# A planned three-engine kernel: the first layer's low product moves from GpSimd to VectorE, with two buffers for low parts, one-bank sums and a new order

## The chip, the cores and the metric

The kernel runs on one core of one Trainium2 chip. The metric is the device time of one execution in microseconds (us), and the time before is the median of three runs. One more execution was recorded by the hardware profiler; its trace is what is read here. The engines are called PE (TensorE, the matrix engine; PEld is its weight load), DVE (VectorE), ACT (ScalarE), POOL (GpSimd) and SP (SyncE, which here issues every DMA).

## What is computed

A causal weighted average over 7 positions (softmax of `weight` for each of 8 heads), then two feed-forward layers of width 2048 over 8192 tokens of 192 values. The first has a rational activation, the second a squared ReLU.

```python
x = attn(x, weight)                       # 7-tap causal average, 2 x 4096 tokens, 192 wide
h = x @ moe_w_in                          # 8192 x 192 @ 192 x 2048
P = a[0] + a[1]*h + a[2]*h*h + a[3]*h*h*h
Q = 1.0 + abs(b[0])*abs(h) + abs(b[1])*h*h
x = (P / (Q + 1e-6)) @ moe_w_out          # 8192 x 2048 @ 2048 x 192
h = x @ moe2_w_in
g = s * relu(h)**2 + b
out = g @ moe2_w_out
```

## The kernel before

**Tiling.** Tokens go in 16 blocks of 512 (`NB`); the 2048 hidden columns go in 8 chunks of 256 (`NPAIR`), so each layer has 16 x 8 = 128 chunks, numbered i (first layer) and j (second). A hidden chunk is a tile of 128 partitions x 2 x 512.

**High and low parts.** Matmuls run in the format fp32r. To keep more digits, each operand is split into a high part (rounded to fp32r) and a low part (what the rounding left). Each chunk of either layer has 10 matmuls into the hidden tile (`mm_in`, L482 to L494) and 10 out of it (`mm_out`, L496 to L503): 6 with the high part of the hidden value and 4 with its low part. Each has 512 columns.

**The first layer's chunk** (`first`, L506 to L607), by engine. PE: `in1`. ACT: `V` (L516), `B` (L530), `S` (L522), `Ln` (L549), `Exp` (L552), which give the numerator's square, the denominator Q and its reciprocal R. DVE: `v` (L540, the numerator; it is the last reader of the hidden PSUM tile and frees it), `hi` (L557, the high part), `m` (L563) and `rest` (L569), which give what the high part missed, multiplied by Q. POOL: `lo` (L575), that remainder times R, which is the low part. PE: `oh` and `ol` (L499) add the high and the low products to the block's sums. The tile `lo` has one buffer, so the `lo` of chunk i waits for the `ol` of chunk i - 1; Q, R and V have three buffers each, and `lo` is the last reader of Q and R.

**The second layer's chunk** (`second`, L671 to L711): `in2` on PE; `relu` (L680), `hi2` (L684) and `Sq` (L687) on ACT; `lo2` (L691, a subtraction) on DVE, into one buffer; `oh2` and `ol2` on PE.

**Between them.** The sums of a block are a PSUM tile of two banks, `acc1` for the first layer and `acc2` for the second, one of each. `middle` (L609 to L668) reads `acc1` and makes the operands of the second layer: `half` (L617) and `middle high` (L626) on ACT, `add` (L632) and `middle low` (L642) on DVE, `mid high` (L650) on ACT, `mid low` (L658) on DVE, one copy by DMA. `finish` (L713 to L747) reads `acc2`: `f1` (L720) and `f0` (L727) on ACT, `other` (L736) on DVE, two stores. The other two hidden tiles `h0` and `h1` take the remaining four of the eight PSUM banks; either layer's `in` takes the one that is free.

**Ahead of it.** For each block the 7 taps (L370, L372) and the split of x (L379, L380, L392, L393) run on DVE and ACT. At the start the 16 weight chunks are loaded as 64-bit floats, read as integer words, and converted to high and low parts (`convert`, L274 to L344) on ACT and DVE. `choose` (L749 to L763) is 14 very short DVE instructions that set a flag: whether the fast form used here holds for the given coefficients. The flag is read at the very end (L931), and a second, general program follows only if it does not hold. While PE has nothing to do at the start it runs 18 + 240 fill matmuls on zeros (L822).

**What sets the order.** Each engine runs its instructions in the order of the program. That order comes from a planner (`Plan.order`, L117 to L166): every step has an engine, a cost and predecessors, and the planner takes, engine by engine, among the steps that can start within `window` of the earliest, the one with the smallest key: chunk number x `PERIOD` plus a constant for its kind (`KEY`). Steps marked `two`, and all POOL steps, also exclude each other in its clock (`port`). So the keys only decide among steps that are ready at nearly the same planned moment. In between, semaphores enforce the dependences of tiles: a reader waits for the last writer of a tile, and a writer for its last readers.

Of the kernel before, what the change touches and what calls it, by code (L numbers as in the profile page):

```python
# [65 lines left out]
PERIOD = 49.3361  # L66
SAME, OTHER, WINDOW = 0.13, 0.18, 0.0346
KEY = {
    "B": -205.47, "Exp": 1361.10, "Ln": -1099.73, "S": 2329.47, "Sq": -1965.35, "V": -35.99,
    "add": 76.87, "again2": 3213.31, "bias": 250.60, "choose": 0.00, "f0": -476.58,  # L70
    "f1": -346.45, "fill": 1302.02, "finish": -1057.72, "flatten": 1033.64, "half": 533.91,
# [4 lines left out]
    "mid low": -600.72, "middle high": 1011.40, "middle low": -55.44, "oh": 399.83,  # L76
    "oh2": 956.49, "ol": 208.83, "ol2": 363.40, "raw": 217.36, "relu": -316.51,
    "rest": -215.80, "rows": 55.35, "store": -645.27, "store2": -35.28, "tap0": 706.19,
# [3 lines left out]
}  # L82
WARM, FILLS = 18, 120
MOST, WORST, SMALL, LARGE = 0.5, 16.0, 1e-6, 1e12
# [85 lines left out]
def conv_rational_relu2(  # L170
# [30 lines left out]
    def part(nm, n):  # L201
        return work.tile([P, 2, NB], F32R, tag=nm, name=nm, bufs=n)

# [292 lines left out]
    def mm_out(acc, W, x, c, terms):  # L496
        for k in range(2):
            for n, (w, m) in enumerate(terms):
                nc.tensor.matmul(  # L499
                    acc[:, m, :], lhsT=W[c][:, w + k * P:w + (k + 1) * P], rhs=x[:, k, :],  # L500
                    start=terms is HIGH and c == 0 and k == 0 and n != 1,
                    stop=terms is LOW and c == NPAIR - 1 and k == 1,
                )  # L503


    def first(i, x_done):  # L506
# [66 lines left out]
        def low(_):  # L573
            lo = a["lo"] = part("lo", 1)
            nc.gpsimd.tensor_tensor(lo, a["q"], a["r"], op=ALU.mult)  # L575

        def out_high(_):
            if c == 0:
                accs[1, blk] = psum("acc1")
# [13 lines left out]
        else:  # L593
# [10 lines left out]
        s_lo = step("lo", i, "Pool", 2.4, i, low, (s_r, ("ol", i - 1)))  # L604
        s_oh = step("oh", i, "PE", 6 * MM, i, out_high,
                    (s_h, ("lows", c), ("middle low", blk - 1) if c == 0 else None))
        return step("ol", i, "PE", 4 * MM, i, out_low, (s_lo, s_oh))  # L607

    def middle(blk, ready):  # L609
# [4 lines left out]
        def half(tag):  # L614
            a["t"] = scratch(tag)[0:D1]
            if fast:
                nc.scalar.activation(  # L617
                    a["t"], accs[1, blk][D1:P, 1, :], AF.Copy, scale=sign[D1:P]
                )
                return  # L620
            nc.scalar.copy(a["t"], accs[1, blk][D1:P, 1, :])

        def high(_):
            X2[blk] = x_tiles(2)
            if fast:
                nc.scalar.activation(X2[blk][0], accs[1, blk][:, 0, :], AF.Copy, scale=sign)  # L626
                return
            nc.scalar.copy(X2[blk][0], accs[1, blk][:, 0, :])

        def add(_):  # L630
            if fast:
                nc.vector.scalar_tensor_tensor(  # L632
                    a["t"], accs[1, blk][0:D1, 1, :], sign[0:D1], a["t"],
# [3 lines left out]
            nc.vector.tensor_add(a["t"], accs[1, blk][0:D1, 1, :], a["t"])  # L637

        def low(_):
            xh, xl, _, _ = X2[blk]  # L640
            if fast:
                nc.vector.scalar_tensor_tensor(  # L642
                    xl, accs[1, blk][:, 0, :], sign, xh.bitcast(F32),
# [3 lines left out]
            nc.vector.tensor_sub(xl, accs[1, blk][:, 0, :], xh.bitcast(F32))  # L647
# [8 lines left out]
        def low2(_):  # L656
# [333 lines left out]
```

## Time and profile before

| | us |
|---|---|
| median of 3 runs (lowest to highest) | 1298.39 (1295.28 to 1298.67) |
| the profiled execution | 1297.07 |
| its span, first to last instruction | 1295.2 |
| PE busy | 1245.9 (96%) |
| ACT busy | 1175.8 (91%) |
| DVE busy | 1087.8 (84%) |
| POOL busy | 382.8 (30%) |

The profiled execution lasts 1.87 us longer than its span and 1.32 us less than the median. Its granted TensorE clock was 0.992 of the full 2.4 GHz on average. A busy share is an average over stages that have different limits, so the stretches are read one by one in the rows below. A matmul's own duration (0.39 us) is longer than the distance at which the next one starts, since matmuls are pipelined; PE is therefore counted in starts. Likewise a DVE or ACT instruction overlaps the next one's start a little, so a group's busy sum is larger than the engine's busy time.

### The profile page before, as it was taken

Reading aid. Unit: us, or ns where it says so; the run is one execution under the profiler, and the core shown is the slowest. Engines: PE = TensorE matmul, PEld = TensorE weight load, DVE = VectorE, ACT = ScalarE, POOL = GpSimd, SP = SyncE. Lnnn points to the kernel's source line nnn. Section 1 sums busy time; section 2 is a strip of 40 time slices with the busy share of each in tenths; the row PEclk is TensorE's granted clock in tenths of the full one; section 3 lists DMA queues with packets and bytes.
Section 4 is the critical chain, followed back from the end, with each engine's and each line's share of the span. In section 5 each row is a group of like instructions: output and inputs, shape, how many; then the busy total and the mean of one; then the engine's idle time right before and its main releaser. Section 6 shows DMA issues by size and latency. Waiting matters only on the chain.

```text
span 1295.2 us, 14466 instructions
## 1 busy us (share of the span) xinstructions
PE 1245.9 (96%) x5405; PEld 985.1 (76%) x5414; DVE 1087.8 (84%) x1038; ACT 1175.8 (91%) x1241; POOL 382.8 (30%) x160
## 2 busy tenths in 40 slices
PE   7989999999999999999989999899999999999997
PEld 3555787788888888787778787787877778888885
DVE  7999998999889989998878778787878887887832
ACT  4989999999999999989979899799979999999864
POOL 1122223324232232323242332433243232323300
PEclk8999999999999999999999999999999999999999
DMA  5410010000000100000000000000000000000000
GB/s 196 183 49 5 1 29 17 13 25 13 6 25 9 29 13 13 25 13 17 9 25 5 13 17 14 21 5 13 17 13 17 1 17 5 17 1 5 13 17 15
DMA packets 12047, 30.32 MB, mean 23 GB/s; under 512 B 1792, under 2 KB 1792, under 8 KB 11968
## 3 DMA queue, kind: packets, MB, share of 16 engines
q1 hardware_dynamic: 11968, 29.32, 7.4%
q8 instruction: 44, 0.72, 0.2%
q14 instruction: 35, 0.29, 0.1%
HBM read 18.96 MB, written 6.29 MB: 19 GB/s over the span
## 4 chain that ended last, share of the span: by engine, by line
PE 60%; ACT 17%; DVE 13%; issue 5%; POOL 4%; DMA 0%; ACTq 0%; DVEq 0%; POOLq 0%
PE acc L499 30%; PE h L490 30%; POOL lo L575 4%; ACT R L549 2%; ACT Q L522 2%; ACT Q L530 2%; ACT hi L684 2%; ACT V L516 2%; DVE V L540 2%; DVE Q L563 2%; DVE hi L557 1%; DVE y L372 1%; DVE Q L569 1%; ACT R L552 1%; ACT G L687 1%
## 5 line engine op out<-in xcount | busy, mean ns | idle before, releaser
L575 POOL TENSOR_TENSOR lo<-Q,R 128x1024 fp32r<-128x1024 f32 x128 | 376.6, 2942 | 848.9 <-PE acc L499 357.2
L499 PE MATMUL acc<-hi,w 128*128 128x512 f32 x1536 | 380.7, 390 | 4.1 <-DVE hi L557 2.4
L499 PEld LDWEIGHTS acc<-hi,w 128*128 128x128 f32 x1536 | 287.4, 188 | 68.2 <-DVE hi L557 4.4
L499 PE MATMUL acc<-lo,w 128*128 128x512 f32 x1024 | 266.9, 392 | 8.0 <-POOL lo L575 6.7
L499 PEld LDWEIGHTS acc<-lo,w 128*128 128x128 f32 x1024 | 191.1, 188 | 54.7 <-POOL lo L575 12.3
L691 DVE TENSOR_TENSOR lo<-G,hi 128x1024 fp32r<-128x1024 f32 x128 | 174.9, 1366 | 54.9 <-PE acc L499 32.8
L557 DVE SCALAR_TENSOR_TENSOR hi<-V,few,R 128x1024 fp32r<-128x1024 f32 x128 | 166.4, 1300 | 49.2 <-PE acc L499 25.1
L540 DVE SCALAR_TENSOR_TENSOR V<-V,few,h 128x1024 f32<-128x1024 f32 x128 | 163.2, 1276 | 51.7 <-ACT Q L530 51.4
L563 DVE SCALAR_TENSOR_TENSOR Q<-Q,few,hi 128x1024 f32<-128x1024 f32 x128 | 190.5, 1488 | 2.5
L490 PE MATMUL h<-x1h,w 128*128 128x512 f32 x512 | 165.4, 405 | 21.0 <-DVE V L540 11.1
L569 DVE SCALAR_TENSOR_TENSOR Q<-V,few,Q 128x1024 f32<-128x1024 f32 x128 | 183.9, 1436 | 0.6
L680 ACT ACTIVATE G<-h 128x1024 f32<-128x1024 f32 x128 | 130.3, 1018 | 41.7 <-PE h L490 27.7
L530 ACT ACTIVATE Q<-h,few 128x1024 f32<-128x1024 f32 x128 | 142.3, 1112 | 28.2 <-POOL lo L575 27.6
L516 ACT ACTIVATE V<-h,few 128x1024 f32<-128x1024 f32 x128 | 153.5, 1199 | 8.3 <-PE h L490 7.7
L490 PE MATMUL h<-x2h,w 128*128 128x512 f32 x512 | 158.5, 391 | 2.6 <-DVE V L540 2.6
L549 ACT ACTIVATE R<-Q,few 128x1024 f32<-128x1024 f32 x128 | 146.9, 1148 | 1.2
L522 ACT ACTIVATE Q<-Q,few 128x1024 f32<-128x1024 f32 x128 | 147.1, 1149 | 0.9
L552 ACT ACTIVATE R<-R,few 128x1024 f32<-128x1024 f32 x128 | 146.9, 1148 | 1.0
L684 ACT ACTIVATE hi<-G 128x1024 fp32r<-128x1024 f32 x128 | 135.4, 1058 | 4.0 <-PE acc L499 3.3
L687 ACT ACTIVATE G<-G 128x1024 f32<-128x1024 f32 x128 | 135.1, 1055 | 0.7
L490 PEld LDWEIGHTS h<-x1h,w 128*128 128x128 f32 x512 | 94.3, 190 | 52.6 <-ACT G L680 11.7
L490 PEld LDWEIGHTS h<-x2h,w 128*128 128x128 f32 x512 | 94.9, 188 | 24.7 <-DVE V L540 3.5
(101 smaller groups left out, 1393.2 us busy)
## 6 DMA issues: line engine op xcount, KB each, us to landing
raw<-w SPq DMA_DIRECT2D x16, 767.8 KB, 7.0
x_in<-xt SPq DMA_DIRECT2D x24, 259.0 KB, 2.7
out<-z SPq DMA_DIRECT2D x16, 256.0 KB, 2.0
x2d<-x2d SPq DMA_DIRECT2D x16, 128.0 KB, 2.2
out<-z SPq DMA_DIRECT2D x16, 128.0 KB, 2.3
x1d<-x1d SPq DMA_DIRECT2D x15, 128.0 KB, 2.2
head<-taps SPq DMA_DIRECT2D x1, 11.0 KB, 1.8
```

The costliest lines, as they stand in the source:

```text
L490: nc.tensor.matmul(h[:, k, :], lhsT=W[c][:, w + k * P:w + (k + 1) * P], rhs=x, start=terms is wide and n == 0, stop=terms is rest and n == ...
L499: nc.tensor.matmul(acc[:, m, :], lhsT=W[c][:, w + k * P:w + (k + 1) * P], rhs=x[:, k, :], start=terms is HIGH and c == 0 and k == 0 and n ...
L516: nc.scalar.activation(a["v"], a["h"], AF.Square, bias=alpha, scale=slope)
L522: nc.scalar.activation(a["q"], a["q"], AF.Square, bias=beta)
L530: nc.scalar.activation(a["q"], a["h"], AF.Abs, scale=root)
L540: nc.vector.scalar_tensor_tensor(v, v, cadd if fast else ab[:, 1:2], a["h"], op0=ALU.add, op1=ALU.mult)
L549: nc.scalar.activation(a["r"], a["q"], AF.Ln, bias=lnb, scale=2.0 ** -QEXP)
L557: nc.vector.scalar_tensor_tensor(hi, a["v"], padd if fast else ab[:, 0:1], a["r"], op0=ALU.add, op1=ALU.mult)
L563: nc.vector.scalar_tensor_tensor(q, q, qadd if fast else qc, a["hi"].bitcast(F32), op0=ALU.add, op1=ALU.mult)
L569: nc.vector.scalar_tensor_tensor(q, a["v"], padd if fast else ab[:, 0:1], q, op0=ALU.add, op1=ALU.subtract)
L575: nc.gpsimd.tensor_tensor(lo, a["q"], a["r"], op=ALU.mult)
L691: nc.vector.tensor_sub(lo, a["g"], a["hi"].bitcast(F32))
```

## The change

- `lo` of every chunk of the first layer is issued on DVE (`nc.vector`) instead of POOL (`nc.gpsimd`), with the planner's cost 1.14 instead of 2.4. POOL then has no work after the start.
- `lo` and `lo2` get two buffers each (`LOWS = 2`), and wait for the `ol` or `ol2` two chunks back instead of one.
- `acc1` and `acc2` become two tiles of one bank each. Their readers' predecessors follow: `middle high` and `half` each wait only for the sums, `add` for `half`, `middle low` for `middle high`, and `f0` no longer waits for `f1`. The first `oh` of a block also waits for `add` of the block before.
- `choose` gets the key of chunk 128 instead of 32, waits for `finish` of block 0, and is registered behind all other steps.
- `PERIOD`, `WINDOW` and all of `KEY` are new, so the planner gives a new order on every queue.

`RELU_ON_DVE` is empty, so `relu` stays on ACT. The general program keeps one buffer and POOL; it gets the one-bank sums too.

```diff
-PERIOD = 49.3361
-SAME, OTHER, WINDOW = 0.13, 0.18, 0.0346
+PERIOD = 153.1447
+SAME, OTHER, WINDOW = 0.13, 0.18, 0.0993
 KEY = {
...
 WARM, FILLS = 18, 120
+LOWS = 2
+RELU_ON_DVE, LOW_ON_DVE = (), (0,1,2,3,4,5,6,7)
...
+    def sums(tag):
+        return [ps.tile([P, NB], F32, tag=f"{tag}{m}", name=f"{tag}{m}") for m in range(2)]
+
     def psum(tag):
         return ps.tile([P, 2, NB], F32, tag=tag, name=tag)
...
         def low(_):
-            lo = a["lo"] = part("lo", 1)
-            nc.gpsimd.tensor_tensor(lo, a["q"], a["r"], op=ALU.mult)
+            lo = a["lo"] = part("lo", LOWS if fast else 1)
+            engine = nc.vector if fast and c in LOW_ON_DVE else nc.gpsimd
+            engine.tensor_tensor(lo, a["q"], a["r"], op=ALU.mult)
 
         def out_high(_):
             if c == 0:
-                accs[1, blk] = psum("acc1")
+                accs[1, blk] = sums("acc1")
             mm_out(accs[1, blk], W1, a["hi"], c, HIGH)
...
-        s_lo = step("lo", i, "Pool", 2.4, i, low, (s_r, ("ol", i - 1)))
+        own = fast and c in LOW_ON_DVE
+        s_lo = step("lo", i, "DVE" if own else "Pool", 1.14 if own else 2.4, i, low, (s_r, ("ol", i - (LOWS if fast else 1))), two=True)
         s_oh = step("oh", i, "PE", 6 * MM, i, out_high,
-                    (s_h, ("lows", c), ("middle low", blk - 1) if c == 0 else None))
+                    (s_h, ("lows", c), *((("add", blk - 1), ("middle low", blk - 1)) if c == 0 else ())))
...
         hs = step("middle high", blk, "ACT", 0.48, when, high,
-                  [t] + [("in2", NPAIR * (blk - 1) + c) for c in range(NPAIR)])
-        ad = step("add", blk, "DVE", 0.6, when, add, (hs,))
-        ls = step("middle low", blk, "DVE", 0.6, when, low, (ad,))
-        h2 = step("mid high", blk, "ACT", 0.52, when, high2, (ad,))
+                  [ready] + [("in2", NPAIR * (blk - 1) + c) for c in range(NPAIR)])
+        ad = step("add", blk, "DVE", 0.6, when, add, (t,))
+        ls = step("middle low", blk, "DVE", 0.6, when, low, (hs,))
+        h2 = step("mid high", blk, "ACT", 0.52, when, high2, (hs, ad))
...
-        s_l = step("lo2", j, "DVE", 1.14, j, low, (s_s, ("ol2", j - 1)), two=True)
+        s_l = step("lo2", j, "DVE", 1.14, j, low, (s_s, ("ol2", j - (LOWS if fast else 1))), two=True)
...
-        f0 = step("f0", blk, "ACT", 0.66, when, most, (f1,), take="scratch")
+        f0 = step("f0", blk, "ACT", 0.66, when, most, (ready, ("bias", 0)), take="scratch")
...
-        if fast:
-            step("choose", 0, "DVE", 2.5, 4 * NPAIR, choose)
         for blk in range(NBLK):
...
+        if fast:
+            step("choose", 0, "DVE", 2.5, NPAIR * NBLK, choose, (("finish", 0),))
         for st in plan.order():
```

## Rows read from the trace of the kernel before

**Rows 1.** Windows: busy us (x instructions) of PE, PEld, DVE, ACT, POOL; clock; DMA.

```profile
22.50:50.00 27.50, 23.04 (x87) 13.56 (x88) 27.02 (x45) 24.92 (x38) 0.92 (x1) 0.84 0.47 178
50.00:100.00 50.00, 45.92 (x196) 27.17 (x198) 49.12 (x61) 45.45 (x60) 14.26 (x6) 1.00 0.24 89
100.00:190.00 90.00, 86.18 (x388) 63.54 (x391) 88.92 (x104) 87.19 (x106) 23.35 (x9) 1.00 0.05 13
300.00:500.00 200.00, 199.80 (x878) 163.77 (x877) 182.80 (x165) 195.18 (x199) 61.13 (x22) 1.00 0.06 15
500.00:1100.00 600.00, 581.75 (x2517) 471.28 (x2516) 492.44 (x441) 551.10 (x559) 196.81 (x63) 0.99 0.05 14
```

**Rows 2.** Chain of waits, PE work without idle time: start, us, what.

```profile
326.49 4.53 PE acc L499 x20
```

**Rows 3.** Line view, PE's fills: count, ns min/median/max, first and last start.

```profile
L822 PE MATMUL acc<-G x249: 379/379/650, 1.2 to 137.7; 128*128 128x512 bf16 x125
```

**Rows 4.** Timeline of DVE at the start: start us, duration us, instruction.

```profile
3.83 0.17 DVE L858 TENSOR_TENSOR head<-head,few 128x14 f32<-128x14 f32 x1
...
10.02 0.48 DVE L370 TENSOR_SCALAR y<-x_in,head 128x512 f32<-128x512 f32 x1
...
16.94 1.01 DVE L306 SCALAR_TENSOR_TENSOR z<-top,z 128x768 int16<-128x768 int16 x1
```

**Rows 5.** Tile view of x_in in the first 40 us: issue to landing.

```profile
DMA to landing us min/median/max: 2.6/2.9/3.3
```

**Rows 6.** Timeline of ACT at the start: the first weight chunk.

```profile
9.41 0.90 ACT L294 ACTIVATE z<-raw 128x768 int32<-128x768 uint32 x1
```

**Rows 7.** Timeline of DVE: a low product of the second layer and its follower.

```profile
198.59 1.22 DVE L691 TENSOR_TENSOR lo<-G,hi 128x1024 fp32r<-128x1024 f32 x1
199.73 1.28 DVE L569 SCALAR_TENSOR_TENSOR Q<-V,few,Q 128x1024 f32<-128x1024 f32 x1
```

**Rows 8.** The page's costliest groups: busy us, mean ns, idle before, its releaser.

```profile
L575 POOL TENSOR_TENSOR lo<-Q,R 128x1024 fp32r<-128x1024 f32 x128 | 376.6, 2942 | 848.9 <-PE acc L499 357.2
...
L691 DVE TENSOR_TENSOR lo<-G,hi 128x1024 fp32r<-128x1024 f32 x128 | 174.9, 1366 | 54.9 <-PE acc L499 32.8
...
L563 DVE SCALAR_TENSOR_TENSOR Q<-Q,few,hi 128x1024 f32<-128x1024 f32 x128 | 190.5, 1488 | 2.5
...
L569 DVE SCALAR_TENSOR_TENSOR Q<-V,few,Q 128x1024 f32<-128x1024 f32 x128 | 183.9, 1436 | 0.6
```

**Rows 9.** Line views of two DVE lines, columns as in group 3.

```profile
L691 DVE TENSOR_TENSOR lo<-G,hi x128: 1204/1220/3207, 142.1 to 1283.4; 128x1024 fp32r<-128x1024 f32 x128
...
L563 DVE SCALAR_TENSOR_TENSOR Q<-Q,few,hi x128: 1266/1280/3472, 45.8 to 1225.7; 128x1024 f32<-128x1024 f32 x128
```

**Rows 10.** Timeline of POOL: a product near the start.

```profile
58.42 2.39 POOL L575 TENSOR_TENSOR lo<-Q,R 128x1024 fp32r<-128x1024 f32 x1 [6.59 <-DVE Q L569]
```

**Rows 11.** Timeline of DVE: the instruction that meets it.

```profile
59.63 2.27 DVE L563 SCALAR_TENSOR_TENSOR Q<-Q,few,hi 128x1024 f32<-128x1024 f32 x1
```

**Rows 12.** Windows of two places, columns as in group 1.

```profile
640.00:680.00 40.00, 35.78 (x149) 28.41 (x148) 30.58 (x30) 33.12 (x35) 14.97 (x4) 0.96 0.10 27
948.00:988.00 40.00, 35.80 (x155) 28.50 (x154) 30.53 (x31) 33.76 (x35) 15.34 (x4) 1.00 0.07 20
```

**Rows 13.** Timeline of POOL: the product in the first of these places.

```profile
653.80 8.12 POOL L575 TENSOR_TENSOR lo<-Q,R 128x1024 fp32r<-128x1024 f32 x1 [11.81 <-ACT R L549]
```

**Rows 14.** Timeline of ACT: who waited for it, idle time in brackets.

```profile
661.95 1.12 ACT L530 ACTIVATE Q<-h,few 128x1024 f32<-128x1024 f32 x1 [4.15 <-POOL lo L575]
```

**Rows 15.** Waits: engine line waited for, us in total, times, longest.

```profile
DVE lo L691 <- PE acc L499: 32.8, 32, 4.1
...
PE h L490 <- DVE V L540: 13.7, 9, 1.9
```

**Rows 16.** Chain of waits at the end: start, us, what.

```profile
1279.54 2.56 PE acc L499 x10
```

**Rows 17.** Timeline of DVE at the end, idle time in brackets.

```profile
1287.54 0.74 DVE L736 SCALAR_TENSOR_TENSOR z<-acc,head,z 64x512 f32<-64x512 f32 x1 [2.91 <-ACT z L727]
```

More of the change, by code (lines that the diff above doesn't have):

```diff
@@ L65 @@
 }
-PERIOD = 49.3361
-SAME, OTHER, WINDOW = 0.13, 0.18, 0.0346
+PERIOD = 153.1447
+SAME, OTHER, WINDOW = 0.13, 0.18, 0.0993
 KEY = {
-    "B": -205.47, "Exp": 1361.10, "Ln": -1099.73, "S": 2329.47, "Sq": -1965.35, "V": -35.99,
-    "add": 76.87, "again2": 3213.31, "bias": 250.60, "choose": 0.00, "f0": -476.58,
-    "f1": -346.45, "fill": 1302.02, "finish": -1057.72, "flatten": 1033.64, "half": 533.91,
[4 rows of a table removed]
-    "mid low": -600.72, "middle high": 1011.40, "middle low": -55.44, "oh": 399.83,
-    "oh2": 956.49, "ol": 208.83, "ol2": 363.40, "raw": 217.36, "relu": -316.51,
-    "rest": -215.80, "rows": 55.35, "store": -645.27, "store2": -35.28, "tap0": 706.19,
[3 rows of a table removed]
+    "B": 2065.15, "Exp": 1765.52, "Ln": -517.70, "S": 110.85, "Sq": -1729.37, "V": 2437.89,
+    "add": 1443.98, "again2": 854.45, "bias": -96.78, "choose": -4317.30, "f0": 2690.75,
+    "f1": -1796.18, "fill": 770.95, "finish": -689.17, "flatten": -3154.65, "half": -320.53,
[4 rows of a table added]
+    "mid low": -246.78, "middle high": -273.37, "middle low": -636.70, "oh": 893.43,
+    "oh2": 2518.06, "ol": 368.02, "ol2": 2702.40, "raw": -276.87, "relu": -2491.34,
+    "rest": 2392.24, "rows": -3516.19, "store": 916.79, "store2": 123.89, "tap0": 1361.44,
[3 rows of a table added]
 }
 WARM, FILLS = 18, 120
+LOWS = 2
+RELU_ON_DVE, LOW_ON_DVE = (), (0,1,2,3,4,5,6,7)
 MOST, WORST, SMALL, LARGE = 0.5, 16.0, 1e-6, 1e12
@@ L617, in half @@
                 nc.scalar.activation(
-                    a["t"], accs[1, blk][D1:P, 1, :], AF.Copy, scale=sign[D1:P]
+                    a["t"], accs[1, blk][1][D1:P], AF.Copy, scale=sign[D1:P]
                 )
                 return
-            nc.scalar.copy(a["t"], accs[1, blk][D1:P, 1, :])
+            nc.scalar.copy(a["t"], accs[1, blk][1][D1:P])
         def high(_):
@@ L625, in high @@
             if fast:
-                nc.scalar.activation(X2[blk][0], accs[1, blk][:, 0, :], AF.Copy, scale=sign)
+                nc.scalar.activation(X2[blk][0], accs[1, blk][0][:], AF.Copy, scale=sign)
                 return
-            nc.scalar.copy(X2[blk][0], accs[1, blk][:, 0, :])
+            nc.scalar.copy(X2[blk][0], accs[1, blk][0][:])
         def add(_):
@@ L636, in add @@
                 return
-            nc.vector.tensor_add(a["t"], accs[1, blk][0:D1, 1, :], a["t"])
+            nc.vector.tensor_add(a["t"], accs[1, blk][1][0:D1], a["t"])
         def low(_):
@@ L646, in low @@
                 return
-            nc.vector.tensor_sub(xl, accs[1, blk][:, 0, :], xh.bitcast(F32))
+            nc.vector.tensor_sub(xl, accs[1, blk][0][:], xh.bitcast(F32))
         def high2(_):
@@ L679, in relu @@
             a["g"] = tmp("G", 2)
+            if fast and c in RELU_ON_DVE:
+                nc.vector.tensor_scalar(a["g"], a["h"], 0.0, None, op0=ALU.max)
+                return
             nc.scalar.activation(a["g"], a["h"], AF.Relu)
@@ L689, in low @@
         def low(_):
-            lo = a["lo"] = part("lo2", 1)
+            lo = a["lo"] = part("lo2", LOWS if fast else 1)
             nc.vector.tensor_sub(lo, a["g"], a["hi"].bitcast(F32))
@@ L694, in out_high @@
             if c == 0:
-                accs[2, blk] = psum("acc2")
+                accs[2, blk] = sums("acc2")
             mm_out(accs[2, blk], W2, a["hi"], c, HIGH)
@@ L702, in second @@
                  list(x_done) + [("weights", NPAIR + c)], take="slot")
-        s_r = step("relu", j, "ACT", 0.9, j, relu,
+        own = fast and c in RELU_ON_DVE
+        s_r = step("relu", j, "DVE" if own else "ACT", 1.14 if own else 0.9, j, relu,
                    (h, ("lo2", j - 2), ("fill", FILLS - 1) if j == 1 else None), free=(h,))
@@ L720, in half @@
             nc.scalar.activation(
-                a["t1"], accs[2, blk][D1:P, 1, :], AF.Identity,
+                a["t1"], accs[2, blk][1][D1:P], AF.Identity,
                 bias=bias2[D1:P, 1:2], scale=ss[D1:P],
@@ L727, in most @@
             nc.scalar.activation(
-                a["t0"], accs[2, blk][:, 0, :], AF.Identity, bias=bias2[:, 0:1], scale=ss
+                a["t0"], accs[2, blk][0][:], AF.Identity, bias=bias2[:, 0:1], scale=ss
             )
@@ L736, in other @@
             nc.vector.scalar_tensor_tensor(
-                t1, accs[2, blk][0:D1, 1, :], ss[0:D1], t1, op0=ALU.mult, op1=ALU.add
+                t1, accs[2, blk][1][0:D1], ss[0:D1], t1, op0=ALU.mult, op1=ALU.add
             )
@@ L817, in conv_rational_relu2 @@
         nc.vector.memset(idle, 0.0)
-        zero = psum("acc2")
+        zero = sums("acc2")[0]
         def fill(n):
@@ L822, in fill @@
                 nc.tensor.matmul(
-                    zero[:, 0, :], lhsT=idle[:, 0:P], rhs=idle, start=True, stop=True
+                    zero, lhsT=idle[:, 0:P], rhs=idle, start=True, stop=True
                 )
```

6 lines of the change are left out of this document (3 added, 3 removed), and 14 rows, old and new, of the table KEY.

## The prediction

> **What bounds the kernel now.** I read the windows first. From 300 to 500 us PE is busy 199.8 of 200 us [rows 1]: there it is the bound. Twenty of its matmuls take 4.53 us [rows 2], so one costs 0.2266 us, and 200 us hold 883. The 5120 matmuls of the two layers (128 chunks x 20 x 2) need 5120 x 0.2266 = 1160 us. No part of the change touches these. So the question is what lies around the 1160 us, in a span of 1295.2.
>
> Two stretches hold most of it. In the head, from 22.5 to 190 us, DVE is the fullest engine: 27.02, 49.12 and 88.92 us busy, which is 165.1 of 167.5 (98.5%) [rows 1]; PE looks busy only because 249 recorded fills run until 137.7 us [rows 3]. The head ends when DVE has converted the weights and served the first blocks. In the steady part, 500 to 1100 us, PE starts 2517 matmuls where 600 / 0.2266 = 2648 would fit: 131 missing, 29.7 us. Its idle time there is 18.3 us [rows 1]; the rest is unrecorded matmuls and a clock below full (0.99). So 18 to 30 us are to be had there.
>
> **Where the steady loss sits.** Two windows of 40 us (of three that look alike, some 154 us apart) start 149 and 155 matmuls instead of 176.5, so they lose 6.2 and 4.9 us [rows 12]; with the third (149, as the first) that is 17.3 us. In the first of them one POOL product takes 8.12 us [rows 13]. ACT waits 4.15 us for it, as the tile Q is not free until then [rows 14]. DVE then gets Q late, PE gets the hidden tile late, and the granted clock of the window is 0.96, while in its like at 948 it stays at 1.00 [rows 12]: the pause costs PE its idle time and in two of three cases some slow matmuls behind it.
>
> **POOL and DVE disturb each other.** A product on POOL runs from 58.42 to 60.81 us [rows 10]. A DVE instruction of line 563 that starts at 59.63 takes 2.27 us [rows 11] where the median is 1.28 [rows 9], and so ends 1.1 us after POOL does. The mean of line 563 is 1.488 against that median: 128 x 0.208 = 26.6 us. Line 691 loses 128 x (1.366 - 1.220) = 18.7, line 569 (same form as 563) 128 x (1.436 - 1.280) = 20.0 [rows 8, 9]. These three lines alone lose 65 us of DVE time to POOL. The 2.9 us that POOL needs per product [rows 8] against 2.39 [rows 10] show the other direction.
>
> **The change part by part.**
>
> *The product on DVE.* The nearest row is line 691: two SBUF inputs, the same shape and types. It takes 1.22 us, and the next instruction starts 1.14 us after it [rows 7]. Bounds: 1.14 and 1.28 (line 563, an instruction with one more operation); I take 1.14. DVE gains 128 x 1.14 = 146 us and loses at least the 65 above: 1088 + 146 - 65 = 1169 us at most, 92% of a span of 1270. PE stays the bound on average, but barely above DVE.
> - In the head there are 1 + 6 + 9 = 16 products [rows 1], +18.2 us on the fullest engine. Each met about one stretched instruction; at the 1.0 us of [rows 11] that returns 16. Net +2 us, bounds 0 (more returned than I count) and +18 (nothing returned).
> - In the steady part DVE has 600 - 492 = 108 us free [rows 1]; 63 products add 72. I put no cost on them; the cover is that idle time, and where it is gone each product costs 1.14 us (the slower rival).
> - The three places above disappear: -17, bounds 0 and -30. What is late next is DVE's line 540, which frees the hidden tile: PE waits for it 9 times, 13.7 us [rows 15]. Some of these waits are in the three places.
>
> *A new wait on DVE.* `lo` needs a buffer that `ol` has left. On POOL that wait (357 us [rows 8]) held up nobody; on DVE, behind it stand line 540, `hi` and the taps. Its likeness is line 691, which with one buffer waits 32.8 us for PE in 32 cases [rows 15]. With two buffers for both, the wait is for the chunk before last; I take 0, bounds -33 and +33 us of DVE idle time, which touches PE only when DVE is the fullest.
>
> *`choose` later.* After line 858 ends at 4.00 us, DVE does nothing but `choose` and its waits until the first tap at 10.02: 6.0 us [rows 4]. The first x tile is issued by 1.2 us or so and lands within 3.3 us [rows 5], so the taps could start at 4.5. The first conversion also needs ACT's line 294, which ends at 10.31 [rows 6], while DVE's join (line 306) starts at 16.94 [rows 4], six taps and more behind. So the head can start 5.5 us earlier. I take -5; bounds 0 (another load is late) and -6. Behind block 0 its 14 short instructions lie in DVE's idle time. If that is missing they cost 3 us; nobody waits for the flag before the end.
>
> *One-bank sums, two buffers at the end.* The last chunks have ten matmuls in 2.56 us instead of 2.27 [rows 2, 16], as the one buffer of `lo2` holds them: with three such chunks, -0.9. The last DVE instruction waits for line 727 [rows 17], which the split lets it pass: -0.8. Bounds 0 and -2. Inside, the split lets line 632 go before 626; it is covered by PE work.
>
> *The new order.* It moves everything on every queue, also SP's loads, copies and stores. Loads of x land in 3 us [rows 5] and a block takes 8 x 20 x 2 x 0.2266 = 72.5 us, so a transfer has room in either order. The rows of before can't show the order itself. What speaks for it: planned costs for DVE are right to a few per cent, while the planner's POOL step (2.4 us) could take 8.12 [rows 13]; without POOL the chip should follow the plan more closely. That the order loses nothing new in the head is an assumption.
>
> **The sum**, against the profiled execution: 1297.07 - 5 (choose) + 2 (head) - 17 (three places) - 1.7 (end) = 1275.4; I say 1275. The median before was 1.3 us above that execution, inside the spread of the runs.
>
> **The rivals.**
> 1. *The order gains more.* All 30 us of the steady loss go, choose gives 6, the head pays nothing, the end 1.7: 1297.1 - 37.7 = 1259. For it: 300 to 500 us already ran without loss with DVE at 91%. Against it: there DVE still had POOL to take the products, and not all of PE's waits for line 540 lie in those three places.
> 2. *The gain is given back in the head.* Only half of the stretches return, as the products fill the places where DVE sat beside POOL: +18.2 - 8 = +10; the steady part saves 4 instead of 17, since the waits for line 540 take over; 1297.1 - 5 + 10 - 4 - 1.7 = 1296. No measurable change.
> 3. *DVE becomes the bound: slower.* DVE's queue is in order. If `lo` stands ahead of line 540, the hidden tile is freed 1.14 us later and PE waits. At two chunks of eight in all blocks that is 32 x 1.14 = 36.5 against the 21.7 of the sum: 1312. It decides from 21.7 / 1.14 = 19 chunks of 128 on. For it: at 300 to 500 us DVE has 17.2 us free [rows 1] and 22 products of 1.14 are 25 us, so without returned stretches it would be over full there; line 540 is already what PE waits for most. Against it: those stretches do return, at least 22 x 65 / 128 = 11 us of them, which leaves DVE at 98% in the densest stretch and well below elsewhere. The Trainium skill (Perfetto Trace Analysis, Optimizing Scalar/DVE Operations) speaks on this side: with DVE saturated, moving some of its work to GpSimd may make sense, and this change does the reverse. The same section doubts the offload between these two because they share a read port, and the stretched row above shows that sharing.
>
> **How the numbers follow.** Forecast (1275, itself between 1264 and 1289): 0.54. Rival 1: 0.17. Rival 2: 0.12. Rival 3: 0.17. About 0.3% (4 us) is what a measurement of this kernel can tell from no change. Faster 0.71, same 0.12, slower 0.17. The range runs from 1255, a little under rival 1, to 1307, short of rival 3's centre: outside lie about half of rival 3 and little below.
>
> **What would show it.** POOL idle behind the first 10 us. Median and mean of lines 563, 569 and 691 equal. `lo` at 1.22 us on DVE. First tap at about 4.5 us, and the fills over by 132 us or so. No window of 40 us between 500 and 1100 that starts fewer than 165 matmuls. DVE busy between 1140 and 1170 us. Wrong it would be if PE's waits for line 540 grow well beyond 13.7 us, if DVE waits for PE in the new `lo` with a queue behind it, or if the head lasts longer with DVE still full.

## The result: 1254.7 us, twice the forecast gain

| | before | after |
|---|---|---|
| median, us | 1297.74 (1295.28 to 1298.67) | 1254.72 (1254.61 to 1255.00) |
| profiled execution, us / span | 1297.07 / 1295.2 | 1254.61 / 1252.7 |
| ratio, 95% interval | | 0.9672 (0.9655 to 0.9688) |
| DVE busy, us | 1087.8 | 1143.6 |
| matmul starts, 500 to 1100 us | 2517 | 2647 |

43 us were gained where 22 were forecast. The direction and the mechanism held; the size did not, and the missing half is the subject of the experiments. Line numbers are higher after the change: `lo` is L581 (575 before), `v` L545 (540), `hi` L562 (557), `m` L568 (563), `rest` L574 (569), `lo2` L701 (691).

The page after, engines first (busy us, share, instructions), then its costliest groups (busy us, mean ns | idle time before), which answer [rows 8]:

```profile
span 1252.7 us, 14124 instructions
...
PE 1231.3 (98%) x5405; PEld 986.6 (79%) x5414; DVE 1143.6 (91%) x1166; ACT 1187.6 (95%) x1241; POOL 13.5 (1%) x32
...
L701 DVE TENSOR_TENSOR lo<-G,hi 128x1024 fp32r<-128x1024 f32 x128 | 155.8, 1217 | 34.6 <-PE acc L504 25.6
L568 DVE SCALAR_TENSOR_TENSOR Q<-Q,few,hi 128x1024 f32<-128x1024 f32 x128 | 163.8, 1280 | 1.8
L574 DVE SCALAR_TENSOR_TENSOR Q<-V,few,Q 128x1024 f32<-128x1024 f32 x128 | 163.7, 1279 | 1.3
...
L581 DVE TENSOR_TENSOR lo<-Q,R 128x1024 fp32r<-128x1024 f32 x128 | 155.7, 1217 | 2.3
```

The means that POOL had stretched to 1366, 1488 and 1436 ns are 1217, 1280 and 1279. `lo` itself takes 1217 ns, and DVE stands idle before it for 2.3 us in all 128 chunks together: the new wait on DVE costs nothing.

The windows after, columns and stretches as in [rows 1]; the fourth line is of a stretch that is not among those rows, where the kernel before starts 469:

```profile
22.50:50.00 27.50, 22.44 (x88) 12.25 (x89) 26.93 (x46) 24.61 (x37) 0.00 (x0) 0.88 0.51 192
50.00:100.00 50.00, 47.86 (x207) 30.49 (x210) 49.65 (x60) 48.13 (x61) 0.00 (x0) 1.00 0.12 45
100.00:190.00 90.00, 87.60 (x396) 65.02 (x397) 89.27 (x110) 87.27 (x103) 0.00 (x0) 1.00 0.05 12
190.00:300.00 110.00, 109.60 (x482) 89.64 (x481) 108.81 (x119) 109.25 (x112) 0.00 (x0) 1.00 0.06 16
300.00:500.00 200.00, 200.00 (x884) 165.44 (x883) 198.77 (x198) 197.23 (x200) 0.00 (x0) 1.00 0.07 19
500.00:1100.00 600.00, 599.90 (x2647) 496.41 (x2646) 557.27 (x520) 587.04 (x588) 0.00 (x0) 1.00 0.05 14
```

From 500 to 1100 us PE starts 2647 matmuls where 2648 fit: the whole loss of 29.7 us is gone, not the 17 of the forecast. The places of [rows 12] are as full as any other stretch:

```profile
640.00:680.00 40.00, 40.00 (x178) 33.14 (x177) 37.89 (x36) 39.24 (x40) 0.00 (x0) 1.00 0.07 20
...
948.00:988.00 40.00, 40.00 (x178) 33.12 (x177) 38.33 (x37) 38.86 (x39) 0.00 (x0) 1.00 0.04 11
```

More was won earlier. The timeline of DVE at the start answers [rows 4] (start, duration, instruction), and the line view of `lo2` (ns min/median/max, first and last start) answers [rows 9]:

```profile
3.65 0.17 DVE L869 TENSOR_TENSOR head<-head,few 128x14 f32<-128x14 f32 x1
4.01 0.48 DVE L375 TENSOR_SCALAR y<-x_in,head 128x512 f32<-128x512 f32 x1 [0.18 <-DMA x_in<-xt]
...
11.69 1.02 DVE L311 SCALAR_TENSOR_TENSOR z<-top,z 128x768 int16<-128x768 int16 x1
```

```profile
L701 DVE TENSOR_TENSOR lo<-G,hi x128: 1202/1217/1228, 130.5 to 1240.6; 128x1024 fp32r<-128x1024 f32 x128
```

The first tap starts at 4.01 instead of 10.02 us, the first join at 11.69 instead of 16.94, and the second layer's first `lo2` at 130.5 instead of 142.1. The 500th weight load of the two layers, counted in the trace (which has all 5120 of them), starts at 193.7 us where it was at 201.0. So the head gives about 7 us, the steady part 29.5, and about 6 lie between 200 and 500 us, behind 1100 and at the end. PE's waits, the part of [rows 15]:

```profile
PE acc L504 <- DVE hi L562: 4.9, 1, 4.9
PE acc L504 <- DVE lo L581: 3.7, 4, 1.6
...
PE h L495 <- DVE V L545: 0.2, 1, 0.2
```

PE waited 13.7 us in 9 cases for line 540 to free the hidden tile; now it waits once, for 0.2 us.

### The profile page after: what moved, and what is told of

It reads as the page before. It is cut to its first block, busy times and chain, and to the rows that moved or that the text cites. A ratio compares the mean times of both kernels' runs of the same rounds, so it can differ in the third digit from the quotient of the medians.

```text
span 1252.7 us, 14124 instructions
## 1 busy us (share of the span) xinstructions
PE 1231.3 (98%) x5405; PEld 986.6 (79%) x5414; DVE 1143.6 (91%) x1166; ACT 1187.6 (95%) x1241; POOL 13.5 (1%) x32
## 4 chain that ended last, share of the span: by engine, by line
PE 85%; DVE 8%; ACT 4%; issue 2%; DMA 0%; SPq 0%; DVEq 0%; ACTq 0%
PE acc L504 43%; PE h L495 42%; DVE y L377 1%; DVE z L311 1%; DVE hi L562 1%; DVE Q L568 1%; DVE Q L574 1%; ACT Q L535 1%; ACT Q L527 1%; ACT V L521 1%; DVE lo L581 1%; DVE V L545 1%; DVE w L331 1%; DVE top L307 0%; ACT R L554 0%
## 5 line engine op out<-in xcount | busy, mean ns | idle before, releaser
L504 PE MATMUL acc<-hi,w 128*128 128x512 f32 x1536 | 391.3, 392 | 5.2 <-DVE hi L562 4.9
L504 PE MATMUL acc<-lo,w 128*128 128x512 f32 x1024 | 272.9, 391 | 3.8 <-DVE lo L581 3.7
L562 DVE SCALAR_TENSOR_TENSOR hi<-V,few,R 128x1024 fp32r<-128x1024 f32 x128 | 163.9, 1281 | 40.0 <-ACT R L557 32.8
L701 DVE TENSOR_TENSOR lo<-G,hi 128x1024 fp32r<-128x1024 f32 x128 | 155.8, 1217 | 34.6 <-PE acc L504 25.6
L568 DVE SCALAR_TENSOR_TENSOR Q<-Q,few,hi 128x1024 f32<-128x1024 f32 x128 | 163.8, 1280 | 1.8
L574 DVE SCALAR_TENSOR_TENSOR Q<-V,few,Q 128x1024 f32<-128x1024 f32 x128 | 163.7, 1279 | 1.3
L545 DVE SCALAR_TENSOR_TENSOR V<-V,few,h 128x1024 f32<-128x1024 f32 x128 | 162.9, 1272 | 0.1
L495 PE MATMUL h<-x1h,w 128*128 128x512 f32 x512 | 160.8, 395 | 0.7 <-ACT G L690 0.4
L581 DVE TENSOR_TENSOR lo<-Q,R 128x1024 fp32r<-128x1024 f32 x128 | 155.7, 1217 | 2.3
```

Source lines behind the costliest of these rows:

```text
L495: nc.tensor.matmul(h[:, k, :], lhsT=W[c][:, w + k * P:w + (k + 1) * P], rhs=x, start=terms is wide and n == 0, stop=terms is rest and n == ...
L504: nc.tensor.matmul(acc[m], lhsT=W[c][:, w + k * P:w + (k + 1) * P], rhs=x[:, k, :], start=terms is HIGH and c == 0 and k == 0 and n != 1, ...
L545: nc.vector.scalar_tensor_tensor(v, v, cadd if fast else ab[:, 1:2], a["h"], op0=ALU.add, op1=ALU.mult)
L562: nc.vector.scalar_tensor_tensor(hi, a["v"], padd if fast else ab[:, 0:1], a["r"], op0=ALU.add, op1=ALU.mult)
L568: nc.vector.scalar_tensor_tensor(q, q, qadd if fast else qc, a["hi"].bitcast(F32), op0=ALU.add, op1=ALU.mult)
L574: nc.vector.scalar_tensor_tensor(q, a["v"], padd if fast else ab[:, 0:1], q, op0=ALU.add, op1=ALU.subtract)
```

## The experiments

Three questions: how much of the gain is the engine and how much the order; what price POOL's work really has; and whether each small part is worth what the sum said. A "frozen" order is one in which every engine keeps the order of the kernel named, so that a difference is that of the edit alone. All ratios are against the kernel before.

**Engine alone, in the order of before.**

```diff
-            nc.gpsimd.tensor_tensor(lo, a["q"], a["r"], op=ALU.mult)
+            (nc.vector if fast else nc.gpsimd).tensor_tensor(lo, a["q"], a["r"], op=ALU.mult)
```

> The kernel before with its order as it is; only the first layer's low product is executed by DVE, at the place in the order where POOL's stood, with one buffer. Theory A: the blocking is gone, so 17 to 30 us less than before, 1268 to 1281 us, although the order was not made for it. Theory B: within 5 us of before or slower, as the order makes DVE meet the product and the one buffer at places that were planned for another engine.

1284.85 us (0.990, 0.9883 to 0.9916): 12 us faster, less than the first theory expected and more than the second. Line view of `lo2`, windows and one wait of PE, columns as above:

```profile
L691 DVE TENSOR_TENSOR lo<-G,hi x128: 1206/1219/1228, 146.1 to 1271.2; 128x1024 fp32r<-128x1024 f32 x128
```

```profile
50.00:100.00 50.00, 44.57 (x181) 26.96 (x184) 49.13 (x67) 42.56 (x57) 0.00 (x0) 0.93 0.24 89
100.00:190.00 90.00, 85.88 (x385) 63.77 (x387) 87.31 (x109) 86.68 (x106) 0.00 (x0) 0.98 0.05 12
...
500.00:1100.00 600.00, 594.40 (x2593) 482.68 (x2592) 546.85 (x520) 570.43 (x578) 0.00 (x0) 1.00 0.05 14
```

```profile
PE h L490 <- DVE V L540: 12.2, 24, 2.9
```

Steady part: 2593 - 2517 = 76 matmuls, 76 x 0.2266 = 17.2 us, which is the -17 of the sum to 0.2 us. The three places give 15.4 of them (174, 173 and 174 starts in their 40 us); that the whole comes so close is in part luck. Head: the first `lo2` comes 4.0 us later (146.1), the 500th weight load 4.3 us later (205.3), and 50 to 190 us start 18 matmuls fewer (4.1 us). The product in the head costs +4 and not +2. And the wait for line 540 stays, which the forecast named as what is late next: 12.2 us in the whole run, 5.6 of them in the steady part, where PE has no other wait left and 55 starts (12.5 us) are still missing.

**All parts, in the order of before.** The product on DVE, two buffers for `lo` and `lo2`, sums in one-bank tiles, `choose` issued behind everything.

```diff
-            lo = a["lo"] = part("lo", 1)
-            nc.gpsimd.tensor_tensor(lo, a["q"], a["r"], op=ALU.mult)
+            lo = a["lo"] = part("lo", 2 if fast else 1)
+            (nc.vector if fast else nc.gpsimd).tensor_tensor(lo, a["q"], a["r"], op=ALU.mult)
...
-            lo = a["lo"] = part("lo2", 1)
+            lo = a["lo"] = part("lo2", 2 if fast else 1)
...
-                accs[1, blk] = psum("acc1")
+                accs[1, blk] = sums("acc1")
...
-            step("choose", 0, "DVE", 2.5, 4 * NPAIR, choose)
+            step("choose", 0, "DVE", 2.5, 4 * NPAIR, lambda _: None)
...
         if fast:
+            choose(None)
             return nc.values_load(flag.bitcast(I32)[0:1], min_val=0, max_val=1)
```

> All parts of the change except the order: the order of the kernel before on every queue, with the product on DVE, two buffers for both low parts, one-bank sums and choose behind everything else. The product alone in this order gave 1284.9. If the parts bring their gain without a new order: choose 5 us at the start, the buffers and banks a few more, 1270 to 1280 us. If the order is what makes use of them: 1280 to 1286 us, and the 30 us down to the changed kernel's 1254.7 are the order's.

1276.62 us (0.9841, 0.9825 to 0.9858). The sum of the prediction, which put the order at nothing, was 1275.4. So all its terms together were right to 1.2 us, in part because errors cancel: the steady part gave 85 starts (19.3 us, where 17 were forecast), the head 0.4 us (500th weight load at 200.6 against 201.0, where 3 were forecast). What was left out is one thing: 1276.62 - 1254.72 = 21.9 us for the order.

```profile
500.00:1100.00 600.00, 596.27 (x2602) 485.03 (x2601) 547.69 (x519) 570.81 (x577) 0.00 (x0) 1.00 0.05 14
```

```profile
PE h L493 <- DVE V L543: 10.8, 16, 3.2
```

In the steady part this kernel starts 2602 matmuls, 45 short of the changed one: 10.2 us. In the head its 500th weight load starts at 200.6 us, against 193.7: 6.9 us. So of the order's 22 us about 10 fall on the steady part and 7 on the head; the others lie between them and behind.

**`choose` placed otherwise in that kernel:** issued with block 0's finish, as the change has it, instead of behind everything.

```diff
+            if fast and blk == 0:
+                choose(None)
...
-            choose(None)
             return nc.values_load(flag.bitcast(I32)[0:1], min_val=0, max_val=1)
```

> All parts of the change except the order, as in the first run of this kind (1276.6), but choose stands behind the finish of block 0 instead of behind everything, where its 2.7 us lay open at the end: 1273 to 1275 us. It is the base for the next kernel.

1276.05 us (0.9835, 0.9819 to 0.9851). The 1 to 3 us expected were not there: 0.6, inside the intervals.

**Engine alone, in the new order.** The changed kernel in its own frozen order, with the product back on POOL.

```diff
-            engine = nc.vector if fast and c in LOW_ON_DVE else nc.gpsimd
+            engine = nc.gpsimd
```

> The changed kernel with its order on every queue as it is (the planner still thinks of the product as DVE work); only the engine that executes the first layer's low product is POOL again. Theory A (POOL's product itself costs the time: it blocks DVE, DVE blocks it, and ACT waits for it): the loss of 500 to 1100 us comes back, 18 to 30 us there and a little in the head, so 1280 to 1300 us, with lines of DVE's two-input instructions stretched again. Theory B (the new order brings the time, the engine matters little): below 1262 us.

1305.93 us (1.0066, 1.0049 to 1.0083): slower than either kernel, and than the first theory expected. Of the 51 us over the changed kernel 14 lie ahead of the 500th weight load (207.6), 16 in 300 to 500 us and 15 in 500 to 1100 us. Its groups (columns as above), one line of the page of before, and one place in the timelines of POOL and DVE:

```profile
L701 DVE TENSOR_TENSOR lo<-G,hi 128x1024 fp32r<-128x1024 f32 x128 | 214.6, 1676 | 55.4 <-PE acc L504 45.2
L562 DVE SCALAR_TENSOR_TENSOR hi<-V,few,R 128x1024 fp32r<-128x1024 f32 x128 | 231.9, 1812 | 19.8 <-ACT R L557 17.4
...
L545 DVE SCALAR_TENSOR_TENSOR V<-V,few,h 128x1024 f32<-128x1024 f32 x128 | 162.8, 1272 | 2.0 <-ACT Q L535 1.9
```

```profile
L557 DVE SCALAR_TENSOR_TENSOR hi<-V,few,R 128x1024 fp32r<-128x1024 f32 x128 | 166.4, 1300 | 49.2 <-PE acc L499 25.1
```

```profile
301.76 2.76 POOL L581 TENSOR_TENSOR lo<-Q,R 128x1024 fp32r<-128x1024 f32 x1 [4.96 <-DVE Q L574]
302.50 3.11 DVE L562 SCALAR_TENSOR_TENSOR hi<-V,few,R 128x1024 fp32r<-128x1024 f32 x1 [0.24 <-ACT R L557]
```

DVE is busy 1191.8 us here with 128 products fewer than the changed kernel's 1143.6. Without them (128 x 1.14 = 146) that one would be busy 998, so POOL stretches DVE by 194 us; in the order of before it was 1087.8 - 998 = 90. The order of before kept POOL's products away from `hi` (line 557: a mean of 1300 ns); the new one lets them meet it (1812). `v`, which reads the hidden tile in PSUM, is not stretched: its mean is 1276 ns before and 1272 here and in the changed kernel. In the row shown `hi` ends 1.09 us after POOL does, late by 1.8 us. The Trainium skill (SBUF — State Buffer, Who interferes with whom) states that a DVE instruction with two SBUF inputs contends with a GpSimd instruction that reads SBUF, that the port pair which they share is an exclusive lock, and that issue order decides who blocks; this row agrees.

Side by side, the kernels show that the two parts don't add:

| product on | order of before | new order |
|---|---|---|
| POOL | 1297 | 1306 (all other parts too) |
| DVE | 1277 (all other parts too), 1285 (alone) | 1255 |

The new order is worth -22 with the product on DVE and costs 9 with it on POOL, although the other parts are then there as well.

**POOL given work that nobody waits for.** The changed kernel, and on POOL in each chunk a read of two columns of Q, which ties it to that moment, and a product of POOL's own tile, the size of `lo`. This adds work.

```diff
...
             engine.tensor_tensor(lo, a["q"], a["r"], op=ALU.mult)
+            if fast:
+                first2 = a["q"][:, 0, 0:2]
+                nc.gpsimd.tensor_tensor(tiny, first2, first2, op=ALU.mult)
+                nc.gpsimd.tensor_tensor(dum, dum, dum, op=ALU.mult)
...
```

> The changed kernel, and beside each product on DVE one multiplication of the same size on POOL over a tile of its own, started by the same event as the product was before; nobody waits for its result (a two-element read of Q goes ahead of it, so Q is held until POOL has come to it). If it is the blocking between POOL and DVE that costs: DVE's busy time rises by 65 to 130 us from 1144, beyond what its idle time of 109 us can take, and the time goes to 1275 to 1310 us. If it was only that ACT and PE waited for POOL's results: at most 1262 us.

1374.77 us (1.059, 1.0572 to 1.0608), beyond the range expected: 120 us slower than the changed kernel for results that are never read. Its engines and two groups of POOL, then one wait of PE and one of ACT, columns as above:

```profile
PE 1269.9 (92%) x5405; PEld 995.2 (72%) x5414; DVE 1284.7 (93%) x1166; ACT 1198.2 (87%) x1241; POOL 532.7 (39%) x289
...
L584 POOL TENSOR_TENSOR tiny<-Q 128x2 f32<-128x2 f32 x128 | 188.4, 1472 | 778.6 <-DVE Q L574 774.9
...
L585 POOL TENSOR_TENSOR dum<-dum 128x1024 f32<-128x1024 f32 x128 | 335.1, 2618 | 0.0
```

```profile
PE h L495 <- DVE V L545: 60.0, 38, 4.1
...
ACT Q L535 <- POOL tiny L584: 1.1, 2, 0.8
```

DVE's busy time grows by 1284.7 - 1143.6 = 141 us with the same 1166 instructions, and PE's wait for `v` from 0.2 to 60.0 us. No data, buffer or wait connects DVE to the product `dum`, so this shows that POOL's work stretches DVE's without any of them, in this order. Two things belong to the price. The two-column read of Q takes POOL another 188.4 us, so the 141 us are the price of both, and the two were not separated. And the read keeps Q a little longer, which cost little: ACT waited for it 1.1 us in all.

**Other keys.** The changed kernel planned with the `PERIOD`, `WINDOW` and `KEY` of before.

```diff
-PERIOD = 153.1447
-SAME, OTHER, WINDOW = 0.13, 0.18, 0.0993
+PERIOD = 49.3361
+SAME, OTHER, WINDOW = 0.13, 0.18, 0.0346
...
```

(and the table `KEY` of before)

> The changed kernel with PERIOD, WINDOW and KEY of before (the planner makes an order from them for the changed steps). Theory A: most of the gain stays, 1255 to 1270 us. Theory B: most of it goes, 1280 to 1300 us.

1325.62 us (1.0219, 1.0196 to 1.0241): 71 us over the changed kernel, beyond both expectations.

```profile
100.00:190.00 90.00, 69.02 (x255) 48.25 (x256) 88.16 (x105) 72.98 (x86) 0.00 (x0) 0.89 0.05 14
...
500.00:1100.00 600.00, 586.83 (x2559) 480.93 (x2558) 546.42 (x516) 561.24 (x568) 0.00 (x0) 0.99 0.05 14
```

255 matmuls instead of 396 from 100 to 190 us: some 32 us lost in this stretch alone (141 x 0.2266), with DVE full. The old keys do not carry over to the new structure: planned anew from them it is even slower than in the order of before kept as it was (1276.62). The order is a part of the change of its own, as large as the engine.

**What the new order does better: two tries.** A candidate was the hidden tile. Measured from the first matmul into it to the end of `v`, worked out from the timelines of PE and DVE for 500 to 1100 us, a first-layer chunk holds it 10.0 us before, 10.0 with all parts in the old order, and 7.3 after. In the order of before `B` starts 3.2 us behind `V` on ACT in the mean (at 608.53 and 611.87 us in one place of the timeline of before), and `v` needs it; in the new one it starts 1.2 us behind. So, first, the kernel with `choose` at block 0 with `B` (L533 there) moved directly behind `V` (L519) or, where it comes later, behind the `lo` that frees its tile, and `v` (L543) following it:

```diff
-        for st in plan.order():
+        order = plan.order()
+        if fast:
+            for i in range(NPAIR * NBLK):
+                sv, sb, su = done["V", i], done["B", i], done["v", i]
+                ahead = [sv] + [done[d] for d in (("lo", i - DEPTH), ("B", i - 1)) if d in done]
+                at = max(order.index(d) for d in ahead) + 1
+                if at < order.index(sb):
+                    order.remove(sb)
+                    order.insert(at, sb)
...
+        for st in order:
```

> The same, and in the order of before one kind of step is moved: ACT's second read of the hidden tile (line 533) stands directly behind the first (line 519), or behind the product that frees its buffer, and DVE's last read (line 543) follows it. In the changed kernel the first layer's hidden tile is held 7.3 us in the mean (500 to 1100 us) against 10.0 in this order. If the new order wins by giving the hidden tiles back sooner: holds below 8.5 us, and most of the 45 matmuls that 500 to 1100 us loses to the changed kernel come back, 1262 to 1268 us. If holds are a by-product and it wins by something else: within 3 us of the kernel beside it, holds shorter or not.

1281.24 us (0.9876, 0.9854 to 0.9899): 5 slower than without the move. The hold fell to 8.2 us, but the steady part only rose from 2602 to 2612 starts, and 190 to 500 us lost 24. PE no longer waits for `v`; it waits for `hi`:

```profile
PE acc L502 <- DVE hi L560: 11.1, 5, 4.6
```

So shorter holds alone don't bring the gain. Second, the other way: the changed kernel with `v` up to three DVE steps later.

```diff
...
+                at = order.index(su)
+                order.remove(su)
+                passed = 0
+                while passed < 3 and order[at] not in stop:
+                    passed += order[at].engine == "DVE"
+                    at += 1
+                order.insert(at, su)
...
```

> The changed kernel with its order, only DVE's last read of the hidden tile (line 545) is moved up to three DVE steps later, as far as the next use of the tile allows; the work is the same. If early release of the hidden tiles is what the new order lives on: holds rise from 7.3 to about 10 us, PE starts to wait for line 545, and the time rises to 1262 to 1290 us. If there is slack enough: within 3 us of 1254.7.

1404.91 us (1.0834, 1.0814 to 1.0855): 150 us over the changed kernel, far beyond both expectations. One wait of PE and one of DVE, a place in the timeline of DVE and a window, columns as above:

```profile
PE h L495 <- DVE V L545: 113.9, 87, 2.4
...
DVE lo L701 <- PE acc L504: 156.3, 90, 4.8
...
645.23 1.23 DVE L701 TENSOR_TENSOR lo<-G,hi 128x1024 fp32r<-128x1024 f32 x1 [4.75 <-PE acc L504]
646.37 1.27 DVE L545 SCALAR_TENSOR_TENSOR V<-V,few,h 128x1024 f32<-128x1024 f32 x1
...
500.00:1100.00 600.00, 536.75 (x2291) 429.61 (x2291) 497.63 (x468) 512.93 (x508) 0.00 (x0) 0.99 0.05 13
```

87 waits of PE, 113.9 us, while DVE is less busy (497.6 of 600 us, against 557.3 in the changed kernel). DVE waits too: 156.3 us in `lo2` for PE (25.6 in the changed kernel). The timeline shows why: the moved `v` stands behind a `lo2` that waits for PE to leave its buffer (directly behind `lo2` in 64 of 128 chunks, in none of the changed kernel), and PE then waits for `v`. The hold rises to 10.8 us, and the price is 150 / 128 = 1.17 us a chunk. This is a relative of the prediction's third rival, in which `v` stands behind `lo`. So a `v` that is late in this way loses the gain, but an early one alone doesn't give it.

**The small parts, each undone in the changed kernel.** `choose` ahead of all planned work, order frozen:

```diff
-            step("choose", 0, "DVE", 2.5, NPAIR * NBLK, choose, (("finish", 0),))
+            step("choose", 0, "DVE", 2.5, NPAIR * NBLK, lambda _: None, (("finish", 0),))
...
+        if fast:
+            choose(None)
         for st in plan.order():
```

> The changed kernel with its order frozen, only the 14 short instructions of choose are issued ahead of all planned work, where they stood before. If the start of the head is worth its time: 1258 to 1261 us (the 5.5 to 6 us by which the first tap comes earlier, or most of it). If the head is set by something else (loads, ACT): within 1 us of 1254.7.

1260.49 us (0.9719, 0.9703 to 0.9735): the later choice is worth 5.8 us; 5 were forecast.

Sums in one tile of two banks, order frozen:

```diff
-        return [ps.tile([P, NB], F32, tag=f"{tag}{m}", name=f"{tag}{m}") for m in range(2)]
+        t = ps.tile([P, 2, NB], F32, tag=tag, name=tag)
+        return [t[:, 0, :], t[:, 1, :]]
```

> The changed kernel with its order frozen, only the sums are again one tile of two banks. My sum gave the split 0.8 us at the end and nothing inside: 1255 to 1257 us. If the new order relies on the split at each of the 31 changes of block (a reader of one half released before the other half's reader is done): 0.7 us or more at each, 1270 us and above.

1255.76 us (0.9682, 0.9666 to 0.9698): 1.0 us; 0.8 were forecast.

One buffer for `lo` and `lo2`. The new order issues a product before the reader of a single buffer, so the order could not be frozen; this one is planned anew with the same keys.

```diff
-LOWS = 2
+LOWS = 1
```

> The changed kernel with one buffer for each low part, planned anew with the same keys (its own order needs the second buffer, so it can't be kept). If the second buffers matter because DVE is nearly full and a wait of the product for PE holds up its whole queue: 1265 to 1290 us, with DVE's waits for PE in both products above 40 us. If they matter only at the end: at most 1258 us. A new plan with keys that were not made for it can cost by itself, so a slow result alone doesn't decide; DVE's waits do.

1273.03 us (0.9815, 0.9799 to 0.9832): 18 us, of the buffer and the other order together. DVE's waits for PE:

```profile
DVE lo L701 <- PE acc L504: 32.6, 20, 7.6
...
DVE lo L581 <- PE acc L504: 18.6, 12, 2.4
```

51.2 us where the changed kernel has 25.6, all of it in `lo2`: the second buffer does remove the wait that the forecast put at nothing. It is also a condition of the new order, which is more than a cost of its own.

**No fills.** The changed kernel, order frozen, without the 240 fill matmuls on zeros (nothing else is left out).

```diff
-            step("fill", n, "PE", 2 * MM, 0, lambda _: fill(2), (warm,))
+            step("fill", n, "PE", 2 * MM, 0, lambda _: None if fast else fill(2), (warm,))
```

> The changed kernel with its order, without the 240 fill matmuls that follow the first 18. They are PE work of 54 us in the head, where DVE and ACT are the full engines. If they only fill idle time: the time stays within 2 us of 1254.7 and the granted clock is the same. If they delay the layers' matmuls that stand behind them: faster, 1240 to 1252 us. If they hold the clock: the granted clock in the first 150 us falls to about half and PE's matmuls get longer there; as PE has some 50 us to spare in the head, 1256 to 1270 us.

1254.73 us (0.9674, 0.9658 to 0.9691): no difference in time. The clock fell as in the third expectation, and the time stayed as in the first.

```profile
22.50:50.00 27.50, 10.15 (x31) 7.17 (x29) 26.93 (x46) 25.47 (x38) 0.00 (x0) 0.75 0.52 196
50.00:100.00 50.00, 37.37 (x133) 27.39 (x134) 49.65 (x60) 47.43 (x60) 0.00 (x0) 0.88 0.11 42
100.00:190.00 90.00, 80.55 (x347) 62.78 (x346) 89.26 (x110) 87.21 (x103) 0.00 (x0) 0.94 0.05 12
```

PE's granted clock is 0.75, 0.88 and 0.94 here, means between its levels of 1.2 and 2.4 GHz (0.88, 1.00 and 1.00 with the fills), and DVE's and ACT's busy time is the same to 0.9 us. So in the head PE is not the bound, and DVE with ACT is, as the prediction read from [rows 1].

## Why the prediction was right, and where it was too small

**POOL and DVE disturb each other: right.** The means of three lines fell to their medians, DVE's busy time came to 1143.6 (1140 to 1170 named), and POOL's idle product showed the coupling with no data between them. The Trainium skill (Perfetto Trace Analysis, Optimizing Scalar/DVE Operations) states that it may make sense to offload work from a saturated DVE, even to GpSimd, and that between these two it might not help, as they share a read port. Here the doubt decides, with the order that goes with it: in the new order the 500th weight load starts at 193.7 us with the product on DVE and at 207.6 with it on POOL, though DVE is nearly full there; in the order of before the head lost by it (205.3 against 201.0). Of the other signs named, the last fill starts at 132.3 us and the emptiest 40 us between 500 and 1100 have 174 starts; only POOL's last instruction ends at 16.2 us and not by 10.

**The three places: right.** -17 was forecast, 17.2 came with the engine alone, 15.4 of it in the places themselves. What was named as late next, the waits for `v`, is the only wait of PE that remained in the steady part (5.6 us there, then 3.7 with all parts).

**The head: a term mis-sized.** The step "+16 returned of 18.2, net +2" gave +4 in the old order. That fewer stretches come back there than the one row of [rows 11] per product says is likely, but no run counts them. Inside its bounds, and small.

**`choose`, buffers, sums, end: right.** 5.8 for 5 and 1.0 for 0.8. The product's wait for its buffer is 0 with two buffers, and 18.6 with one.

**The new order: the step that failed.** The text said that the rows of before can't show it, took no gain for it, and called it an assumption that it "loses nothing new in the head". It is worth 21.9 us, half of the result: about 10 in the steady part, about 7 in the head. The prediction had an argument in hand (an order planned with POOL's 2.4 us, where the chip took up to 8.12), but used it only to say that the term isn't a loss. It did not ask what the order of before had given up for POOL. What the runs show of that: it kept POOL's products out of the way of `hi` (90 us of stretch instead of 194), and with POOL gone an order without that care is 22 us better. That the care itself cost the 22 us is my reading; no run shows it move by move, and to drop the care is not enough, as the order planned from the old keys without POOL shows (1325.62). A term that the trace can't show should have had as its bound all the loss that it could remove: in the steady part what was left over (30 - 17 = 13 us, of which the order took 10). For the head, where it took 7, the rows of before give no bound, and a zero was not worked out from them either. The forecast's own range (1264 to 1289) does not reach 1275 - 13 = 1262.

Rival 1 describes the result best: all 30 us of the steady loss, 6 for `choose`, the end. It is too high by nearly 5 us (1259.4): the head gave 7 where it counts 6, and some lie outside the stretches that it counts. The argument against it, that not all waits for line 540 lie in the three places, is true in the old order (10.8 us remain in the whole run with all parts) and void in the new one (0.2).

**The third rival** did not come, as PE's waits for `v` went to 0.2 us. Its price of 1.14 us a chunk was not tested as it stands; the nearest case, `v` up to three steps later and often behind a waiting `lo2`, cost 1.17 us a chunk.

**What stays open.** Which property of the new order gives the 22 us. A later release of the hidden tile loses, and an earlier one in the old order didn't help; the old keys in the new structure lose 71. The orders differ in every queue, and no single move among those tried carries the gain. It is also not shown that this gain needs the product on DVE: no run has keys made anew for the kernel with POOL, so part of the 22 us may come from better keys as such.

## What to carry to other kernels

When two engines block each other, price the work of the one in lost time of the other (here 90 to 194 us of DVE for 128 products that DVE does in 146), and compare that with doing the work there, even if that engine is nearly full. Busy time alone does not decide it: in the order of before DVE became busier by the move (1141.6 us for 1087.8), and the kernel still gained 12 us, as the three places went, each with one POOL product of 8.12 us (at 653.8, 808.0 and 962.2 us). An order that was planned around such a conflict is part of its cost: change the engine and the order together, and price each with the other frozen, as here -12, +9 and -43 don't add. If a term of a sum can't be read from the trace, give it the bound of all the loss that it could remove, not a zero.

## What the runs showed of the hardware

- POOL work whose results nobody reads, 128 products of 2.62 us and 128 two-column reads of 1.47 us, lengthened DVE's unchanged instructions by 141 us and the kernel by 120 us.
- DVE's `v`, which has one of its two tensors in PSUM, kept its mean of 1272 ns beside POOL's products (the kernel with the product back on POOL), while `hi`, with both in SBUF, went from 1281 to 1812.
- How much POOL costs DVE depends on the order as much as on POOL's time: 90 and 194 us for the same 128 products (377 us and 376 us busy).
- A lower granted clock of TensorE (0.75 from 22.5 to 50 us, 0.88 to 100) in a stretch bound by DVE and ACT cost nothing: 1254.73 against 1254.72 us.
